# Streaming-window attention and channel mix in one kernel: which units' q and k the crossbar turns, q loaded in 1 KB rows, and new orders

## The chip, the cores and the metric

The kernel runs on one core of one Trainium2 chip. The metric is device time in microseconds (us) of one execution. TensorE (PE) does the matrix products, VectorE (DVE) and ScalarE (ACT) the elementwise work, GpSimd (POOL) small copies and casts. SyncE (SP) issues nearly all DMAs (transfers). PSUM is the memory that PE writes to, in banks; SBUF holds everything else.

## The reference

Two layers, one behind the other. Batch is 4, with 8 heads of width 64 over a sequence of 768, so the model width is 512.

```
scores = q @ k.T / sqrt(64)
keep   = (key < 4) | ((0 <= query - key) & (query - key < 128))
a      = softmax(scores where keep)
x      = a @ v                                   # heads side by side: (4, 768, 512)
x_prev = x shifted by one position, zero at the start
xk     = mu_k * x + (1 - mu_k) * x_prev
xr     = mu_r * x + (1 - mu_r) * x_prev
out    = sigmoid(xr @ w_r) * (relu(xk @ w_k) ** 2 @ w_v)    # w_k: 512 x 1024, w_v: 1024 x 512
```

All inputs and the output are float32; the kernel computes in bf16.

## The kernel before

**Units.** The work is cut into 12 units: unit `u` is batch `u // 3` and 256 positions, T = `u % 3`. For each unit the kernel loads q, k and v, casts them to bf16, turns q and k so that the head width lies on the partitions, makes the scores of two heads at a time (a "chunk"; four chunks), takes the exponential, multiplies by a mask, multiplies by v, divides, mixes with the shifted position, and runs the three products of the channel mix one unit later.

**q and k.** Each is loaded by two DMAs of 256 KB into a float32 buffer (`ks`, `qs`, three of each). There are two ways on from there.

- By PE (the units that are not in `KD` for k, or `QD` for q). The load is in rows of 1 KB: a partition gets four positions that follow one another, as the cut `(w l) (p j) d -> w p l (j d)` with `j=4` says (line 334). After the cast (line 540) PE turns each half of the unit in four 128 x 128 products with an identity (line 573) into a PSUM bank, and ACT or DVE copies the bank to `kt` or `qt` (line 586). That copy reads PSUM with a stride, so that positions come out in order.
- By the crossbar (units in `KD` or `QD`). The load is in rows of 256 bytes, one position per partition (line 314). After the cast (line 533) a transposing DMA for each half, issued by SP, writes `kt` or `qt` (line 559). Nothing is left to PE, ACT or DVE.

If the name stands in `ROWS4`, a unit of the second kind is loaded and cast like one of the first (line 334, 540) and turned by the crossbar; its positions then lie out of order in `qt`, and `block` (line 275) gives the scores a view of it that steps over them: 64 x 4 positions, of which the inner four are 128 elements (256 bytes) apart. Before, `ROWS4` is empty.

**Readers.** `scores` (line 718) uses `kt` as the stationary operand and `qt` as the moving one. The sink scores (line 693) read `qt` too. `sink_keys` (line 667, POOL) copies the first four keys of a batch.

**Other lines.** 498 to 504: casts of the weights; 643: casts of v to `vb`; 772: exponential; 786: mask; 805: values; 819 and 822: division; 846 and 855: turn of x by PE and its copy, units 9 to 11 by transposing DMA (866); 874 and 885: the mix (`td`, `xk`, `xr`); 936: product with w_k; 946, 950: relu; 960, 964: square (`kk`); 976, 982: gate and tanh (`th`); 994, 1003: product with w_v and the output tile `ob`; 906 and 916: the same for the last 128 positions; 1010 and 921: stores. 1014 is a product of a zero tile (`warm`), a "fill": its result is used by nobody.

**What sets the order.** Nothing is scheduled when the kernel is built. Each step is recorded in `P.op` with a number; `ORDER` is a list of these numbers, in which a negative number stands for a fill; `CHOICE` names the engine of every step that can run on more than one; `SLOTS` says which buffer of its pool each tile takes. Each engine runs its instructions strictly in the order in which `ORDER` gives them, POOL and the DMAs in SP's queue too.

Of the kernel before, what the change touches and what calls it, by code (L numbers as in the profile page):

```python
# [18 lines left out]
    90: "ACT", 91: "ACT", 92: "ACT", 93: "ACT", 95: "ACT", 97: "ACT", 99: "ACT", 100: "DVE",  # L19
    103: "DVE", 108: "DVE", 109: "POOL", 111: "DVE", 112: "ACT", 113: "ACT", 139: "DVE", 142:  # L20
    "DVE", 144: "DVE", 145: "DVE", 148: "DVE", 151: "DVE", 154: "DVE", 196: "POOL", 199: "POOL",
    202: "POOL", 206: "DVE", 223: "DVE", 227: "DVE", 228: "ACT", 278: "DVE", 283: "DVE", 284:
    "POOL", 287: "ACT", 288: "DVE", 300: "DVE", 309: "ACT", 313: "ACT", 320: "DVE", 356: "DVE",
    358: "POOL", 363: "POOL", 366: "ACT", 367: "ACT", 369: "DVE", 389: "ACT", 446: "DVE", 447:
    "ACT", 527: "DVE", 548: "ACT", 552: "ACT", 555: "DVE", 560: "ACT", 595: "DVE", 597: "DVE",
    600: "POOL", 602: "DVE", 605: "ACT", 606: "DVE", 628: "ACT", 636: "ACT", 677: "POOL", 681:
    "DVE", 683: "DVE", 684: "DVE", 702: "ACT", 706: "ACT", 710: "ACT", 714: "ACT", 753: "DVE",
    759: "DVE", 761: "ACT", 782: "DVE", 783: "ACT", 787: "ACT", 791: "ACT", 795: "ACT", 832:
    "DVE", 838: "ACT", 839: "ACT", 859: "ACT", 866: "DVE", 867: "ACT", 906: "POOL", 912: "DVE",
    914: "ACT", 915: "DVE", 931: "ACT", 935: "ACT", 939: "ACT", 943: "ACT", 1000: "DVE", 1004:  # L30
    "DVE", 1005: "ACT", 1008: "DVE", 1009: "ACT", 1028: "DVE", 1037: "ACT",
}

KD = range(4, 12)
QD = range(8, 12)
# [13 lines left out]
ROWS4 = ()  # L49
# [134 lines left out]
def kernel(  # L184
# [14 lines left out]
    nc = tc.nc  # L199
# [14 lines left out]
    P = Plan()  # L214
# [164 lines left out]
    warm = tile1([128, 256], BF16, "warm")  # L379
# [689 lines left out]
```

## Time and profile before

| | |
|---|---|
| runs | 167.81, 171.39 and 171.40 us; median 171.39 us |
| profiled execution, first to last instruction (the span) | 167.6 us |
| PE, DVE, ACT, POOL busy | 159.7, 146.2, 133.4, 16.6 us |
| DMA | 34.60 MB in 79042 packets, of which 67112 are under 512 bytes |
| fills (line 1014) | 44 of 512 columns, 13.8 us busy |
| transposing DMAs | 16 of k, 8 of q, 6 of x |

A busy PE is not a PE at its peak: matmuls are pipelined, and the page models their ends. Two things tell more: the pace of a burst of equal matmuls in the chain of waits (the work that ended last, followed back from the end), and the idle time before each group of instructions.

### The profile page before, as it was taken

To read this page: it belongs to the slowest core of one execution; us is meant where nothing else is said; L and a number is where in the kernel's file an instruction comes from. 1 tells how busy PE (TensorE), PEld (TensorE's weight loads), DVE (VectorE), ACT (ScalarE), POOL (GpSimd) and SP (SyncE) were. 2 spreads that over 40 slices of the span, in tenths; PEclk is the share of its full clock that TensorE was granted. 3 is DMA by queue.
4 is the path that set the end of the run, shared out by engine and by line. 5 is a ranking of instruction groups with operands and counts; after the bars stand their busy time and mean duration, and the time that the engine had idled before them with its cause. 6 is when DMAs were issued, how large, how long until landed. Compare 5 with 4: busy or idle time off the path is not lost.

```text
span 167.6 us, 4210 instructions
## 1 busy us (share of the span) xinstructions
PE 159.7 (95%) x1601; PEld 102.4 (61%) x1601; DVE 146.2 (87%) x375; ACT 133.4 (80%) x221; POOL 16.6 (10%) x43
## 2 busy tenths in 40 slices
PE   6999997999999999899999999999999999999991
PEld 1447574755558576676556885665765576764850
DVE  5189999999999999899999999989798799998821
ACT  4269998999999997999879999989799829614340
POOL 6423021005000010022000000010010000000000
PEclk9999999999999999999999999999999999999999
DMA  4999989999899999979999999999997774131303
GB/s 102 300 327 369 346 172 312 372 324 328 189 248 166 204 294 224 253 153 133 218 256 149 214 239 174 233 219 200 211 189 185 194 162 155 63 66 63 125 0 125
DMA packets 79042, 34.60 MB, mean 206 GB/s; under 512 B 67112, under 2 KB 73520, under 8 KB 79024
## 3 DMA queue, kind: packets, MB, share of 16 engines
q1 hardware_dynamic: 79008, 34.35, 92.0%
q8 instruction: 12, 0.20, 0.5%
q14 instruction: 6, 0.05, 0.1%
q10 hardware_dynamic: 16, 0.00, 0.0%
HBM read 24.12 MB, written 6.29 MB: 181 GB/s over the span
## 4 chain that ended last, share of the span: by engine, by line
PE 58%; DVE 11%; DMA 11%; SPq 7%; ACT 7%; issue 3%; ACTq 0%; DVEq 0%
PE bank L936 18%; PE bank L994 18%; PE bank L976 8%; DMA vs<-in_v_dram 6%; SPq L334 5%; PE sc L718 4%; PE bank L805 4%; DMA qs<-in_q_dram 3%; ACT e L772 3%; DMA qt<-qb 2%; DVE ob L1003 2%; DVE e L786 2%; PE bank L846 2%; DVE x L822 2%; PE bank L573 2%
## 5 line engine op out<-in xcount | busy, mean ns | idle before, releaser
L936 PE MATMUL bank<-xk,wk_sb 128*128 128x256 bf16 x384 | 48.1, 273 | 0.1
L994 PE MATMUL bank<-wv_h,kk 128*128 128x512 bf16 x184 | 46.4, 379 | 0.0
L772 ACT ACTIVATE e<-sc 128x1024 bf16<-128x1024 f32 (+1 forms) x48 | 45.4, 974 | 1.2 <-PE sc L718 1.2
L936 PEld LDWEIGHTS <-wk_sb 128*128 128x128 bf16 x384 | 36.2, 98 | 7.6 <-issue 0.7
L786 DVE TENSOR_TENSOR e<-e,mask 128x1024 bf16<-128x1024 bf16 (+1 forms) x48 | 30.7, 655 | 0.7 <-ACT e L772 0.5
L946 ACT ACTIVATE rl<-bank 128x512 bf16<-128x512 f32 x38 | 22.4, 616 | 8.6 <-PE bank L936 8.5
L994 PEld LDWEIGHTS <-kk 128*128 128x128 bf16 x184 | 16.6, 98 | 14.4 <-issue 0.3
L976 PE MATMUL bank<-wr_sb,xr 128*128 128x512 bf16 x96 | 23.8, 379 | 0.0
L885 DVE SCALAR_TENSOR_TENSOR xr<-td,mu_all,xt 128x256 bf16<-128x256 bf16 x48 | 22.5, 482 | 0.0
L885 DVE SCALAR_TENSOR_TENSOR xk<-td,mu_all,xt 128x256 bf16<-128x256 bf16 x48 | 21.3, 477 | 0.1
L964 ACT ACTIVATE kk<-rl 128x512 bf16<-128x512 bf16 x26 | 16.7, 649 | 5.3 <-DVE rl L950 5.3
L822 DVE TENSOR_TENSOR x<-bank,rec 128x256 bf16<-128x256 f32 x48 | 19.2, 416 | 0.3
L1003 DVE SCALAR_TENSOR_TENSOR ob<-th,bank 128x512 f32<-128x512 f32 x23 | 15.7, 681 | 4.2 <-PE bank L994 3.3
L805 PEld LDWEIGHTS <-e 128*128 128x128 bf16 x352 | 14.4, 97 | 5.8 <-DVE e L786 1.0
L805 PE MATMUL bank<-vb,e 128*128 128x65 bf16 x352 | 16.9, 193 | 0.8 <-DVE e L786 0.8
L982 ACT ACTIVATE th<-bank 128x512 f32<-128x512 f32 x24 | 14.3, 616 | 3.6 <-PE bank L976 3.5
L1014 PE MATMUL bank<-warm 128*128 128x512 bf16 x44 | 13.8, 440 | 1.5 <-DVE warm L1032 1.1
L718 PE MATMUL sc<-qt,kt 64*128 64x128 bf16 (+1 forms) x256 | 13.9, 237 | 0.3 <-DMA qt<-qb 0.2
L976 PEld LDWEIGHTS <-xr 128*128 128x128 bf16 x96 | 8.9, 98 | 8.6
L718 PEld LDWEIGHTS <-kt 64*128 64x128 bf16 x256 | 9.3, 94 | 4.5 <-issue 3.0
L874 DVE TENSOR_TENSOR td<-xt 128x512 bf16<-128x512 bf16 x24 | 10.1, 425 | 0.8 <-ACT xt L855 0.8
L855 ACT COPY xt<-bank 128x512 bf16<-128x512 bf16 x15 | 9.1, 608 | 1.8 <-PE bank L846 1.8
(72 smaller groups left out, 157.9 us busy)
## 6 DMA issues: line engine op xcount, KB each, us to landing
vs<-in_v_dram SPq DMA_DIRECT2D x24, 256.0 KB, 5.0
ks<-in_k_dram SPq DMA_DIRECT2D x24, 256.0 KB, 5.6
qs<-in_q_dram SPq DMA_DIRECT2D x24, 256.0 KB, 5.1
out_dram<-ob SPq DMA_DIRECT2D x23, 256.0 KB, 2.9
w<-in_moe_w_k_dram SPq DMA_DIRECT2D x2, 1024.0 KB, 7.3
w<-in_moe_w_v_dram SPq DMA_DIRECT2D x2, 1024.0 KB, 8.6
w<-in_moe_w_r_dram SPq DMA_DIRECT2D x1, 1024.0 KB, 7.1
kt<-kb SPq DMA_TRANSPOSE x16, 4.1
```

The costliest lines, as they stand in the source:

```text
L718: nc.tensor.matmul(out=sc[:, a, o0:o1], lhsT=lhs[rows], rhs=rhs[rows], start=u not in BIAS, stop=True, skip_group_check=u in BIAS)
L772: nc.scalar.activation(out=buf[ek][:, :, lo:], in_=buf[sck][:, :, lo:], func=AF.Exp, scale=scale)
L786: nc.vector.tensor_tensor(out=at, in0=at, in1=m, op=ALU.mult)
L805: nc.tensor.matmul(out=o[:, g, a, :], lhsT=e[:, a, e0:e0 + 128], rhs=rhs, start=(T == 0 and i == 0), stop=(i == len(blocks) - 1), skip_gro ...
L822: P.op("DVE", dve(256), lambda ok=ok, rk=rk, c=c: nc.vector.tensor_tensor(out=buf["x", u][:, :, 128 * c:128 * c + 128].rearrange("p g (a d ...
L885: nc.vector.scalar_tensor_tensor(out=buf[key][:, c, :], in0=buf[tk][:, i, :], scalar=mu[w][:, c:c + 1], in1=xt[:, c, t0 - 1:t0 + 255], op0 ...
L936: nc.tensor.matmul(out=ps[:, i, :], lhsT=wk_sb[:, c, 128 * f:128 * f + 128], rhs=xk[:, c, :], start=(c == 0), stop=(c == NC - 1), skip_gro ...
L946: nc.scalar.activation(out=buf[rk], in_=buf[psk].rearrange("p (i t) -> p i t", i=2), func=AF.Relu)
L964: nc.scalar.activation(out=buf["kk", u][:, 2 * f2:2 * f2 + 2, :], in_=buf[rk], func=AF.Square)
L976: nc.tensor.matmul(out=buf[psk], lhsT=buf["xr", u][:, c, 128 * g:128 * g + 128], rhs=wr_sb[:, c, :], start=(c == 0), stop=(c == NC - 1))
L994: nc.tensor.matmul(out=buf[psk], rhs=wv_h[:, f, :], lhsT=buf["kk", u][:, f, 128 * g:128 * g + 128], start=(f == 0), stop=(f == NF - 1))
L1003: P.op("DVE", dve(512), lambda psk=psk, tk=tk, bk=bk: nc.vector.scalar_tensor_tensor(out=buf[bk], in0=buf[tk], scalar=1.0, in1=buf[psk], o ...
```

## The change

- `KD` goes from units 4 to 11 to units 8 to 11, and `QD` from 8 to 11 to 4 to 11. So k of units 4 to 7 is turned by PE, and q of units 4 to 7 by the crossbar. The numbers of crossbar turns and of PE turns stay the same.
- `ROWS4` goes from empty to `("q",)`: q of units 4 to 11 is loaded in 1 KB rows, turned by the crossbar, and read with the stride by the scores (line 718, 722 in the new file) and the sink scores.
- Fills can now be short: a number from -5 to -8 stands for one of 128 columns. There are 6 of 512 columns and 86 of 128.
- `ORDER`, `SLOTS` and `CHOICE` are new. The first loads now stand in the order k0, q0, v0 (first half), q1, v0 (second half), k1, q2, k2 and v1 by turns, w_k, w_r, k3, q3, v2, w_v. Before, w_k stood ahead of the last load of k2 and of v1.
- By `CHOICE`, POOL casts k 20 times (before 3), q 15 times (7), v 16 times (4), and all of w_k and half of w_r (before none; ACT cast all of w_k). ACT casts k 3 times (15), q 6 (7), v 5 (11), and copies `kt` 12 times (6) and `qt` 5 (14). DVE casts k once (6), q 3 times (10), v 3 times (9), copies `kt` 4 times (2), `qt` 3 (2) and `xt` 5 (3), and does 5 relus (10).

In the new file the lines of the kernel's function stand 4 further down; the fill is at line 1019.

```diff
 CHOICE = {
-    90: "ACT", 91: "ACT", 92: "ACT", 93: "ACT", 95: "ACT", 97: "ACT", 99: "ACT", 100: "DVE",
...
+    90: "POOL", 91: "POOL", 92: "POOL", 93: "POOL", 94: "POOL", 96: "ACT", 97: "ACT", 98: "ACT",
...
-KD = range(4, 12)
-QD = range(8, 12)
+KD = range(8, 12)
+QD = range(4, 12)
...
-ROWS4 = ()
+ROWS4 = ("q",)
...
 ORDER = (
...
 SLOTS = (
...
+        banks = self.pools["bank"]
         for i in ORDER:
             if i < 0:
-                self.fill(self.pools["bank"][-1 - i])
+                self.fill(banks[(-1 - i) % len(banks)], 512 if -i <= len(banks) else 128)
             else:
                 self.ops[i]["emit"]()
...
-    P.fill = lambda bank: nc.tensor.matmul(out=bank, lhsT=warm[:, 0:128], start=True,
-                                           rhs=warm.unsqueeze(1).to_broadcast([128, 2, 256]),
-                                           stop=True)
+    def zeros(bank, n):
+        nc.tensor.matmul(out=bank[:, 0:n], lhsT=warm[:, 0:128], start=True, stop=True,
+                         rhs=warm.unsqueeze(1).to_broadcast([128, 2, 256]) if n == 512 else
+                         warm[:, 0:n])
+
+    P.fill = zeros
```

What the flag `ROWS4` switches on stands in both files:

```
def block(name, u, c, g=None):
    t = buf[name + "t", u]
    if not walked(name, u):
        return t[:, c, :, :] if g is None else t[:, c, g, :]
    t = t.rearrange("p c g t -> p (c g t)").rearrange(
        "p (h j t w) -> p h w t j", h=2, j=4, w=2)[:, c % 2, c // 2]
    return t if g is None else t[:, 32 * g:32 * g + 32]
```

More of the change, by code (lines that the diff above doesn't have):

```diff
@@ L18 @@
 CHOICE = {
-    90: "ACT", 91: "ACT", 92: "ACT", 93: "ACT", 95: "ACT", 97: "ACT", 99: "ACT", 100: "DVE",
[L20 to L30, printed above, removed]
@@ L31 @@
-    "DVE", 1005: "ACT", 1008: "DVE", 1009: "ACT", 1028: "DVE", 1037: "ACT",
-}
-KD = range(4, 12)
-QD = range(8, 12)
+    90: "POOL", 91: "POOL", 92: "POOL", 93: "POOL", 94: "POOL", 96: "ACT", 97: "ACT", 98: "ACT",
+    106: "DVE", 108: "DVE", 109: "DVE", 139: "POOL", 144: "DVE", 145: "POOL", 148: "POOL", 193:
+    "POOL", 196: "POOL", 199: "POOL", 202: "POOL", 205: "DVE", 206: "DVE", 224: "ACT", 228:
+    "ACT", 232: "ACT", 236: "ACT", 275: "POOL", 278: "POOL", 280: "DVE", 281: "POOL", 283:
+    "DVE", 284: "POOL", 286: "DVE", 293: "DVE", 312: "DVE", 317: "ACT", 321: "ACT", 356: "POOL",
@@ new lines @@
+    359: "POOL", 361: "POOL", 364: "POOL", 369: "DVE", 385: "ACT", 389: "ACT", 392: "DVE", 393:
+    "ACT", 436: "POOL", 439: "POOL", 441: "POOL", 443: "DVE", 444: "POOL", 465: "ACT", 473:
+    "ACT", 516: "POOL", 519: "POOL", 526: "ACT", 548: "ACT", 552: "ACT", 556: "ACT", 595:
+    "POOL", 597: "DVE", 598: "POOL", 600: "POOL", 603: "POOL", 605: "ACT", 608: "DVE", 628:
+    "ACT", 632: "ACT", 636: "ACT", 675: "POOL", 677: "DVE", 679: "POOL", 681: "POOL", 683:
+    "ACT", 684: "ACT", 686: "DVE", 710: "ACT", 714: "ACT", 755: "POOL", 757: "POOL", 762: "DVE",
@@ L37 @@
+    774: "DVE", 787: "ACT", 791: "ACT", 830: "POOL", 834: "POOL", 836: "POOL", 839: "ACT", 854:
+    "DVE", 859: "ACT", 866: "DVE", 906: "POOL", 908: "DVE", 910: "POOL", 935: "ACT", 939: "ACT",
+    943: "ACT", 996: "DVE", 1005: "ACT", 1009: "ACT",
+}
+KD = range(8, 12)
+QD = range(4, 12)
 XD = (9,10,11)
```

164 rows, old and new, of tables (ORDER, SLOTS) are left out of this document.

## The prediction

> **What bounds the kernel now.** I read the busy times first, then the stretches of time, then the chain of waits.
>
> ```profile
> span 167.6 us, 4210 instructions
> PE 159.7 (95%) x1601; PEld 102.4 (61%) x1601; DVE 146.2 (87%) x375; ACT 133.4 (80%) x221; POOL 16.6 (10%) x43
> ```
>
> PE looks full, but fills and modelled ends are in that. So I work out what its real work needs, from the pace of bursts in the chain (start, length, what) and the counts of the groups.
>
> ```profile
> L936 PE MATMUL bank<-xk,wk_sb 128*128 128x256 bf16 x384 | 48.1, 273 | 0.1
> L994 PE MATMUL bank<-wv_h,kk 128*128 128x512 bf16 x184 | 46.4, 379 | 0.0
> L976 PE MATMUL bank<-wr_sb,xr 128*128 128x512 bf16 x96 | 23.8, 379 | 0.0
> L805 PE MATMUL bank<-vb,e 128*128 128x65 bf16 x352 | 16.9, 193 | 0.8 <-DVE e L786 0.8
> ```
>
> ```profile
> 12.91 10.07 DMA vs<-in_v_dram
> ...
> 29.64 0.62 PE sc L718 x12
> ...
> 50.64 2.18 PE bank L936 x20
> ...
> 59.51 0.44 PE sc L718 x12
> ...
> 81.59 0.69 DVE ob L1003
> ...
> 97.03 5.09 DMA qs<-in_q_dram
> ...
> 140.01 0.48 PE bank L805 x16
> ...
> 148.68 1.73 PE bank L994 x8
> ...
> 163.89 0.42 DVE ob L916
> ```
>
> One product of 936 takes 2.18 / 20 = 0.109 us, one of 994 or 976 1.73 / 8 = 0.216, one of 805 0.48 / 16 = 0.030, one of 718 0.44 / 12 = 0.037. With the counts: 384 x 0.109 = 41.9, 280 x 0.216 = 60.5, 352 x 0.030 = 10.6, and 256 scores x 0.037 = 9.5. The 168 turns of 128 columns, at the 0.43 ns a column of line 936 (109 ns / 256), make 9.2; for the 116 small products left I put 5. PE needs 137 us of the 167.6. Where are the other 30?
>
> ```profile
> 0.00:12.00 12.00, 10.47 (x53) 4.42 (x54) 5.81 (x22) 4.77 (x8) 5.95 (x24) 1.00 0.84 242
> 12.00:20.00 8.00, 7.92 (x107) 5.27 (x105) 7.65 (x22) 7.89 (x12) 1.57 (x2) 1.00 1.07 362
> 24.00:30.00 6.00, 4.90 (x76) 3.25 (x76) 5.96 (x18) 5.30 (x10) 1.83 (x3) 1.00 0.96 289
> 30.00:60.00 30.00, 30.00 (x317) 19.44 (x312) 29.57 (x75) 29.69 (x52) 2.85 (x5) 1.00 1.13 257
> 80.00:107.00 27.00, 26.79 (x292) 17.59 (x290) 26.30 (x73) 25.12 (x43) 0.00 (x0) 1.00 1.24 211
> 131.00:164.00 33.00, 32.85 (x276) 21.05 (x272) 27.38 (x66) 16.15 (x28) 0.00 (x0) 1.00 0.36 103
> ```
>
> (Columns: stretch, length, busy PE, PE weight load, DVE, ACT, POOL, granted clock, DMA share, GB/s.) And what PE did up to 29.6 us:
>
> ```profile
> L936 PE MATMUL bank<-xk,wk_sb 128*128 128x256 bf16 x32 | 3.8, 272 | 0.0
> L805 PE MATMUL bank<-vb,e 128*128 128x65 bf16 x56 | 2.9, 194 | 0.8 <-DVE e L786 0.8
> L718 PE MATMUL sc<-qt,kt 64*128 64x128 bf16 (+1 forms) x40 | 2.3, 239 | 0.0
> ```
>
> Up to 29.64 that is 32 x 0.109 + 56 x 0.030 + 40 x 0.037 and about 4 of turns: 11 us. **The start** loses 19: v of unit 1, behind w_k in the queue, lands only at 12.91 + 10.07 = 23.0, and then DVE has no idle time (5.96 of 6). **The middle**, 29.64 to 163.9, has 126 us of work in 134.3, so 8 are lost, in a stretch in which DVE (29.57 of 30, 26.30 of 27) and ACT are full as well. **The tail** is 3.7. From 131 on PE alone sets the time.
>
> **The change, part by part.**
>
> *Turns.* PE makes 96 turns of q and k before and after, ACT and DVE copy 24 halves, the crossbar turns 24: no term. Sixteen loads go from 256-byte to 1 KB rows. They are 16 x 0.262 = 4.2 MB; at the 211 GB/s of 80 to 107 that is 19.9 us of the queue, at the 362 of 12 to 20, where long rows prevail, 11.6. Up to 8 us of DMA time go, of which the chain shows 5.1 (q at 97). I count this in the middle, below.
>
> *Fills.* 44 x 0.216 = 9.5 us before, 6 x 0.216 + 86 x 0.055 = 6.0 after, all while PE waits for q, k or DVE: 0. If the shorter ones didn't hold the granted clock (1.00 above), the 11 us of the start would double and reach into the dense part; I allow 3 us for this in the range.
>
> *The start.* v of unit 1 goes from the 17th and 18th place in SP's queue, with two DMAs of 1 MB ahead, to the 14th and 16th with none: 16 x 0.262 = 4.2 MB, which the queue has moved at about 15.6 us (12 us x 242 and 3.6 x 362 GB/s). It waits for nothing then. Late next are the weights and DVE. The second half of w_k ends at 6.3 MB, 21.4 us, and POOL has to cast it. No row shows POOL with 1024 elements; two casts of 512 bound it.
>
> ```profile
> 23.90 0.62 POOL L643 CAST vb<-vs 128x512 bf16<-128x512 f32 x1 [8.07 <-DMA vs<-in_v_dram]
> 25.02 0.81 POOL L643 CAST vb<-vs 128x512 bf16<-128x512 f32 x1
> 25.27 1.09 DVE L786 TENSOR_TENSOR e<-e,mask 128x1024 bf16<-128x1024 bf16 x1
> 39.04 1.70 DVE L786 TENSOR_TENSOR e<-e,mask 128x1024 bf16<-128x1024 bf16 x2
> 39.18 1.02 POOL L540 CAST qb<-qs 128x512 bf16<-128x512 f32 x1 [13.35 <-DMA qs<-in_q_dram]
> ```
>
> So 1.24 to 2.04 us each, the last at 24 to 26, unit 0's product done by about 27. Behind these casts in POOL's queue stand half of w_r and k and q of unit 3, which wait some 6 us; PE has unit 1's product in that time, if DVE has made its `xk`. By the built order DVE has fewer casts and relus ahead of unit 1's last `xk`: adding the durations of their rows, 23.2 us against 27.2. DVE operations overlap by about a tenth, so that is 3.5 less. But POOL now makes 11 short casts and the four long ones up to there, against 6 short; the next part prices these at 0.14 and 0.4, so 2.3 come back. That leaves 1 us, and PE has 0.4 more work done at that point. **-1.4**; from -4 (DVE unhindered) to +1.
>
> *The engines in the middle.* Rows that price the moves:
>
> ```profile
> L643 ACT CAST vb<-vs 128x512 bf16<-128x512 f32 x11 | 7.0, 648 | 1.0 <-DMA vs<-in_v_dram 1.0
> L643 DVE CAST vb<-vs 128x512 bf16<-128x512 f32 x9 | 3.8, 421 | 0.0
> L855 ACT COPY xt<-bank 128x512 bf16<-128x512 bf16 x15 | 9.1, 608 | 1.8 <-PE bank L846 1.8
> L586 ACT COPY qt<-bank 128x512 bf16<-128x512 bf16 x14 | 8.7, 630 | 0.9 <-PE bank L573 0.9
> L855 DVE COPY xt<-bank 128x512 bf16<-128x512 bf16 x3 | 1.2, 415 | 0.0
> L586 DVE COPY qt<-bank 128x512 bf16<-128x512 bf16 x2 | 1.4, 680 | 0.0
> L786 DVE TENSOR_TENSOR e<-e,mask 128x1024 bf16<-128x1024 bf16 (+1 forms) x48 | 30.7, 655 | 0.7 <-ACT e L772 0.5
> ```
>
> DVE loses 18 casts (0.42) and five relus, and gains five copies: 9 us less. ACT loses 19 casts (0.65), four of weights and five copies net, and gains five relus: 16 less. POOL gains 37 casts of 512 and five of 1024. They are not free for DVE: where the cast at 39.18 ran, the pair of masks took 1.70, and the mask at 25.27 took 1.09, against a mean of 0.655; other casts stretched nothing. Over the 13 casts behind the first 10 us I count 1.8 us of stretched DVE operations, 0.14 for each. 42 x 0.14 = 5.9 us come back, so DVE gains about 3 and ACT the full 16. [...] I take **-2.5** of the 8 lost: DVE stays as full, while ACT and DMA waits go. Range 0 to -6.
>
> *The stride.* Units 4 to 11 have six with T > 0 (four chunks x 512 columns, two heads side by side) and two with T = 0 (4 x 384); that they do run side by side shows in the 0.44 us for 2048 columns. With six sink scores of 256 the path holds 16,900 columns read with a step of 256 bytes. No row shows PE with a stride. The nearest are the copies of line 586, which read bf16 from PSUM with a step, against line 855 without: ACT 630 against 608, or 0.04 ns an element; DVE 680 against 415, or 0.52. That is 0.7 us or 8.8 us. [...]
>
> Sum: 167.6 - 1.4 - 2.5 + 0.7 = 164.4 us of span. The runs before lay 0.2 (once) and 3.8 us (twice) above the span, so the same would be 164.6 to 168.2; I put down the middle, 166.4.
>
> **Rivals.**
>
> *The stride costs PE (slower).* PE's moving read behaves as DVE's: 8.8 in place of 0.7, so 164.4 + 8.1 = 172.5 of span, 3% slower. Half of it, 168.1, is within 2%; from about 7.2 on it is slower. [...] Against: the ACT row. Chance 0.28.
>
> *POOL's casts make DVE the bound.* At 0.4 each, 42 casts cost 17 us for the 9 saved: 8 us more DVE. It decides where DVE is full, 30 to 107 us, in which about two thirds of the casts fall: 167.6 + 5.3 - 1.4 + 0.7 = 172.2 at the worst, 169.4 at a cost of 0.3. [...] Against: the mean of 0.14. Chance 0.22.
>
> *The relief is worth more.* The lost 8 us fall to 2 as ACT, DMA and DVE all get room, and the start gains 3: 167.6 - 6 - 3 + 0.7 = 159.3. For it: 5.1 us of DMA and the ACT pieces in the chain between 64 and 107. Against: DVE as full as before. Chance 0.15.
>
> My forecast has 0.35. Some 2% is about what a measurement of this kernel can tell from no change, and 164.2 of span is the line to faster. Faster: half the forecast, the third rival and a little of the others, 0.36. Slower: 0.6 of the first rival, half of the second, and some of a new order gone wrong: 0.32. Within 2%: 0.32. Range: 160 (third rival, runs close to the span) to 174.5 (first rival with 2 us between span and run).
>
> **What would show it.** Bursts of 12 scores of units 4 to 11 at 0.44 to 0.6 us say that the stride is free; near 0.9 that it halves the pace. POOL busy should be about 50 us, the mean mask under 0.75, DVE's total near 145, ACT's near 117. v of unit 1 should land before 18 us, and unit 1's first product of line 940 start before 30. A granted clock under 1.00 before 30 us, DVE over 150 us, or PE idle behind a POOL cast of q or k would make the forecast wrong.

## The result, and the profile after

| | before | after |
|---|---|---|
| median of four runs each | 171.02 us | 194.46 us |
| ratio after / before, 95% interval | | 1.151 [1.139, 1.164] |
| span of the profiled execution | 167.6 us | 194.0 us |
| PE, DVE, ACT, POOL busy | 159.7, 146.2, 133.4, 16.6 us | 182.7, 149.9, 124.2, 47.3 us |
| DMA packets (of these under 512 bytes) | 79042 (67112) | 66756 (50728) |

The change made the kernel 15% slower. The ratio is of runs in the faster of two states alone, and three of the four runs of before lie about 3 us above the fourth, so it is not the quotient of the medians. The prediction said 166.4 us, with a range up to 174.5.

The first page of the profile of after:

```profile
span 194.0 us, 4324 instructions
PE 182.7 (94%) x1649; PEld 109.5 (56%) x1649; DVE 149.9 (77%) x355; ACT 124.2 (64%) x199; POOL 47.3 (24%) x85
```

PE has 23 us more of busy time, while DVE's share fell from 87% to 77% and ACT's from 80% to 64%. So PE itself became slower somewhere. The groups of PE's instructions, each shape apart (shapes and count, then busy us and mean ns of one, then idle time before them), show where. First before:

```profile
L718 PE MATMUL sc<-qt,kt 64*128 64x256 bf16 x96 | 11.6, 272 | 0.3 <-DMA qt<-qb 0.2
L718 PE MATMUL sc<-qt,kt 64*128 64x128 bf16 x160 | 11.1, 216 | 0.0
L693 PE MATMUL bank<-qt,ksink 128*32 128x256 bf16 x32 | 2.3, 282 | 0.6 <-ACT rl L946 0.6
```

The same three groups after:

```profile
L722 PE MATMUL sc<-qt,kt 64*128 64x256 bf16 x96 | 23.5, 500 | 0.3 <-ACT qt L590 0.2
L722 PE MATMUL sc<-qt,kt 64*128 64x128 bf16 x160 | 21.9, 344 | 0.0
L697 PE MATMUL bank<-qt,ksink 128*32 128x256 bf16 x32 | 5.4, 627 | 0.0
```

The counts are the same, the means of the scores are 1.8 and 1.6 times as long, that of the sink scores 2.2 times. These are the products that read q, and they do not wait longer: the idle time before a group is 0.6 us at most before, and 0.3 after. A mean hides that a third of them are of units 0 to 3, read as before. The timeline of PE (start, length, what) shows a burst of the changed units by itself; first one of before, then two of after, with T > 0 (12 products) and with T = 0 (8):

```profile
59.34 0.60 PE L718 MATMUL sc<-qt,kt 64*128 64x256 bf16 x12
```

```profile
62.85 1.92 PE L722 MATMUL sc<-qt,kt 64*128 64x256 bf16 x12
84.29 1.48 PE L722 MATMUL sc<-qt,kt 64*128 64x256 bf16 x8
```

A burst of 12 takes three times as long, although the time of its last product alone, 0.22 and 0.39 us, is in both. Units 4 to 11 have 12 such bursts of 12 and 4 of 8.

The second thing to see is in the start. Stretches of time of after (length, busy PE, PE weight load, DVE, ACT, POOL, granted clock, DMA share, GB/s):

```profile
24.00:30.00 6.00, 3.58 (x60) 2.96 (x58) 5.87 (x10) 2.43 (x5) 4.40 (x6) 1.00 1.14 333
30.00:60.00 30.00, 29.06 (x285) 18.95 (x284) 28.27 (x63) 25.04 (x41) 10.36 (x17) 1.00 0.78 210
60.00:80.00 20.00, 19.63 (x158) 9.99 (x158) 15.46 (x36) 13.48 (x23) 3.35 (x7) 0.91 0.96 220
```

From 24 to 30 us DVE is busy for 5.87 of 6 us, yet it has only 10 instructions there; before it had 18 in 5.96. Its timeline in this stretch, and POOL's beside it:

```profile
23.38 1.56 DVE L790 TENSOR_TENSOR e<-e,mask 128x1024 bf16<-128x1024 bf16 x1
24.86 0.47 DVE L889 SCALAR_TENSOR_TENSOR xk<-td,mu_all,xt 128x256 bf16<-128x256 bf16 x1
25.26 1.25 DVE L889 SCALAR_TENSOR_TENSOR xr<-td,mu_all,xt 128x256 bf16<-128x256 bf16 x1
26.43 1.52 DVE L790 TENSOR_TENSOR e<-e,mask 128x1024 bf16<-128x1024 bf16 x1
```

```profile
22.30 2.09 POOL L508 CAST wk_sb<-w 128x1024 bf16<-128x1024 f32 x2 [2.07 <-DMA w<-in_moe_w_k_dram]
25.03 2.38 POOL L508 CAST wk_sb<-w 128x1024 bf16<-128x1024 f32 x2 [0.63 <-DMA w<-in_moe_w_k_dram]
```

The casts end at 24.39 and 27.41. The masks end at 23.38 + 1.56 = 24.94 and 26.43 + 1.52 = 27.95: both times 0.55 us after the cast. Each of these two masks seems to stand still until the cast is over and then to do its work. Between the two pairs of casts an `xk` takes 0.47, and the `xr` that meets the next cast takes 1.25. The page's group of masks hardly shows this (0.718 us for 0.655 before):

```profile
L790 DVE TENSOR_TENSOR e<-e,mask 128x1024 bf16<-128x1024 bf16 (+1 forms) x48 | 33.3, 718 | 4.7 <-ACT e L776 4.7
```

### The profile page after: what moved, and what is told of

The parts are those of the page before. It is cut to its first block, busy times and chain, and to the rows that moved or that the text cites. A ratio compares the mean times of both kernels' runs of the same rounds, so it can differ in the third digit from the quotient of the medians.

```text
span 194.0 us, 4324 instructions
## 1 busy us (share of the span) xinstructions
PE 182.7 (94%) x1649; PEld 109.5 (56%) x1649; DVE 149.9 (77%) x355; ACT 124.2 (64%) x199; POOL 47.3 (24%) x85
## 2 busy tenths in 40 slices
DMA packets 66756, 34.63 MB, mean 178 GB/s; under 512 B 50728, under 2 KB 61232, under 8 KB 66736
## 4 chain that ended last, share of the span: by engine, by line
PE 73%; DVE 17%; ACT 3%; DMA 3%; issue 2%; SPq 1%; DVEq 0%; ACTq 0%
PE bank L998 19%; PE bank L940 17%; PE sc L722 15%; PE bank L980 9%; PE bank L809 5%; DVE e L790 4%; DVE xk L889 3%; DVE xr L889 3%; DMA qs<-in_q_dram 3%; DVE x L826 2%; PE bank L697 2%; PE bank L1019 1%; DVE td L878 1%; PE bank L850 1%; PE bank L577 1%
## 5 line engine op out<-in xcount | busy, mean ns | idle before, releaser
L950 ACT ACTIVATE rl<-bank 128x512 bf16<-128x512 f32 x43 | 25.0, 600 | 24.8 <-PE bank L940 23.9
L790 DVE TENSOR_TENSOR e<-e,mask 128x1024 bf16<-128x1024 bf16 (+1 forms) x48 | 33.3, 718 | 4.7 <-ACT e L776 4.7
L722 PE MATMUL sc<-qt,kt 64*128 64x128 bf16 (+1 forms) x256 | 33.7, 402 | 0.3 <-ACT qt L590 0.2
L998 PEld LDWEIGHTS <-kk 128*128 128x128 bf16 x184 | 17.3, 99 | 19.6 <-issue 3.4
L889 DVE SCALAR_TENSOR_TENSOR xr<-td,mu_all,xt 128x256 bf16<-128x256 bf16 x48 | 24.4, 536 | 0.0
L889 DVE SCALAR_TENSOR_TENSOR xk<-td,mu_all,xt 128x256 bf16<-128x256 bf16 x48 | 23.2, 512 | 0.5
L722 PEld LDWEIGHTS <-kt 64*128 64x128 bf16 x256 | 11.3, 103 | 19.4 <-issue 14.8
L647 POOL CAST vb<-vs 128x512 bf16<-128x512 f32 x16 | 11.4, 718 | 44.5 <-DMA vs<-in_v_dram 44.0
L823 DVE RECIPROCAL rec<-bank 128x4 f32<-128x4 f32 x48 | 7.9, 174 | 16.3 <-PE bank L809 15.9
L1007 DVE SCALAR_TENSOR_TENSOR ob<-th,bank 128x512 f32<-128x512 f32 x23 | 15.7, 682 | 6.0 <-PE bank L998 2.8
L544 POOL CAST qb<-qs 128x512 bf16<-128x512 f32 x15 | 9.8, 668 | 28.5 <-DMA qs<-in_q_dram 14.2
L809 PEld LDWEIGHTS <-e 128*128 128x128 bf16 x352 | 12.9, 97 | 6.1 <-DVE e L790 2.8
```

The costliest lines, as they stand in the source:

```text
L722: nc.tensor.matmul(out=sc[:, a, o0:o1], lhsT=lhs[rows], rhs=rhs[rows], start=u not in BIAS, stop=True, skip_group_check=u in BIAS)
L790: nc.vector.tensor_tensor(out=at, in0=at, in1=m, op=ALU.mult)
L809: nc.tensor.matmul(out=o[:, g, a, :], lhsT=e[:, a, e0:e0 + 128], rhs=rhs, start=(T == 0 and i == 0), stop=(i == len(blocks) - 1), skip_gro ...
L889: nc.vector.scalar_tensor_tensor(out=buf[key][:, c, :], in0=buf[tk][:, i, :], scalar=mu[w][:, c:c + 1], in1=xt[:, c, t0 - 1:t0 + 255], op0 ...
L950: nc.scalar.activation(out=buf[rk], in_=buf[psk].rearrange("p (i t) -> p i t", i=2), func=AF.Relu)
L998: nc.tensor.matmul(out=buf[psk], rhs=wv_h[:, f, :], lhsT=buf["kk", u][:, f, 128 * g:128 * g + 128], start=(f == 0), stop=(f == NF - 1))
```

## The experiments

Two theories came out of this: the strided read costs PE, and POOL's casts cost DVE. The ratios are against runs of the kernel before on the same chip; their median lay between 168.65 and 169.2 us.

**1. The changed kernel without the stride.** `block` reads 256 neighbouring columns, all else as it was, so the scores are of other rows of q.

```diff
-        "p (h j t w) -> p h w t j", h=2, j=4, w=2)[:, c % 2, c // 2]
-        return t if g is None else t[:, 32 * g:32 * g + 32]
+        "p (h w t) -> p h w t", h=2, w=2)[:, c % 2, c // 2]
+        return t if g is None else t[:, 128 * g:128 * g + 128]
```

> The changed kernel, in which the scores and sink scores of units 4 to 11 read 256 neighbouring columns of qt in place of the strided view (the positions are then out of order, so the output is not the reference's; all instructions, loads, casts, turns and orders stay). Theory 1, the strided read is most of the loss: in the trace of the changed kernel a burst of 12 scores takes 1.52 us with the stride and 0.40 without, one of 8 1.08 against 0.29, and a sink score of 256 columns 0.44 against 0.11; 12 x 1.12 + 4 x 0.79 + 6 x 0.33 = 18.6 us come back, so about 175 us (172 to 177). Theory 2, POOL's casts and the new order hold it back and PE would only wait elsewhere: 185 us or more.

Measured: 174.96 us, ratio 1.039 [1.032, 1.047]. Its bursts:

```profile
66.46 0.61 PE L722 MATMUL sc<-qt,kt 64*128 64x256 bf16 x12
77.53 0.50 PE L722 MATMUL sc<-qt,kt 64*128 64x256 bf16 x8
```

The stride costs 194.46 - 174.96 = 19.5 us. The rows say about the same: 12 x (1.92 - 0.61) + 4 x (1.48 - 0.50) = 19.6 for the scores, and some 3 for the sink scores (5.4 us busy, 2.3 here); PE's busy time fell by 22.3, from 182.7 to 160.4, so about 3 of it cost no time. But 4% stay that the stride does not explain.

**2. The kernel before with the stride in units 8 to 11 alone.**

```diff
-ROWS4 = ()
+ROWS4 = ("q",)
```

> The kernel before with ROWS4 = ("q",) alone: q of units 8 to 11 in 1 KB rows and read with the stride, order, engines and k as before. Six bursts of 12, two of 8 and three sink scores become strided: 6 x 1.12 + 2 x 0.79 + 3 x 0.33 = 9.3 us. Theory 1 (each strided column is paid in full on PE's path): 176 to 181 us. Theory 2 (PE has slack in which half or more of it goes under, and the loss of the change is its order): under 175 us.

Measured: 179.73 us, ratio 1.067 [1.061, 1.072]. Four strided units, with their rows of 1 KB, cost 11.1 us in the order of before, in which POOL casts little. So the new order is not needed for the loss.

**3. Rows of 1 KB alone**: the same, but with the contiguous read of experiment 1, hence other rows of q.

> The kernel before, with q of units 8 to 11 in 1 KB rows as in the third experiment (179.73 us), but the scores read 256 neighbouring columns, so that the result is of permuted rows: the rows alone, in the order of before, without the stride. Theory 1 (the chain's 5.1 us DMA wait for q at 97 us is worth something): 1.5 to 4 us faster than before, ratio 0.975 to 0.99. Theory 2 (the wait is covered by other work that comes later anyway, as the 1.4 us between 1 KB and 256-byte rows in the changed kernel suggests): within 1.4 us of before, ratio 0.99 to 1.008. If it is slower by more than 1%, 1 KB rows cost something themselves.

Measured: 171.45 us, ratio 1.011 [0.999, 1.024]. The gain of 1.5 to 4 us that theory 1 expected isn't there. Whether the rows cost something in that order isn't settled by this interval. The ratio of experiments 2 and 3, 1.067 / 1.011 = 1.055, leaves 9.3 us to the stride of four units, which is the 9.3 worked out ahead of experiment 2.

**4. Eight patterns in one kernel.** In the changed kernel each of units 4 to 11 reads `qt` with another step, so the scores are of other elements of q. It ran once, in 186.0 us; only its bursts are read.

```diff
+        if u in (6, 9):
+            n = {6: 2, 9: 4}[u]
+            t = t.rearrange("p (x w i) -> p w x i", w=2, i=n)[:, w]
...
+        s = {4: 2, 5: 4, 7: 8, 8: 16, 10: 64, 11: 128}[u]
+        t = t.rearrange("p (x s) -> p s x", s=s)[:, s // 2 * w:s // 2 * w + s // 2]
```

> The changed kernel in which each unit from 4 to 11 reads qt with another pattern, 256 columns out of the same 512 (the output is not the reference's): step 4 bytes (unit 4), 8 bytes (5), pairs of neighbours 8 bytes apart (6), 16 bytes (7), 32 bytes (8), runs of four neighbours 16 bytes apart (9), 128 bytes (10), 256 bytes (11). Read from the pace of the bursts, 0.42 ns a column without a stride and 1.73 with 256 bytes. Theory A (a line of 16 bytes needs two hits): steps of 4 and 8 bytes and both runs keep 0.42, steps of 16 and more take 1.73. Theory B (two bf16 come in one word of 4 bytes): every step costs at once, 4 bytes already 0.83 or more, pairs and runs less than steps. Theory C (the cost grows with the step): 16 to 128 bytes lie between.

PE's timeline. The rows are, in this order, units 4, 5, 6, 7, 8, 9 and 10: a step of 4 bytes, of 8 bytes, pairs of neighbours 8 bytes apart (a T = 0 unit, 8 products), steps of 16 and of 32 bytes, runs of four neighbours 16 bytes apart (T = 0), and a step of 128 bytes.

```profile
55.76 0.63 PE L730 MATMUL sc<-qt,kt 64*128 64x256 bf16 x12
...
66.67 1.08 PE L730 MATMUL sc<-qt,kt 64*128 64x256 bf16 x12
...
78.49 0.52 PE L730 MATMUL sc<-qt,kt 64*128 64x256 bf16 x8
...
89.26 1.97 PE L730 MATMUL sc<-qt,kt 64*128 64x256 bf16 x12
...
108.13 2.01 PE L730 MATMUL sc<-qt,kt 64*128 64x256 bf16 x12
...
122.55 0.52 PE L730 MATMUL sc<-qt,kt 64*128 64x256 bf16 x8
...
132.88 1.90 PE L730 MATMUL sc<-qt,kt 64*128 64x256 bf16 x12
```

Beside 0.61 and 0.50 of the contiguous read, three patterns are free, or nearly so: those in which every 16 bytes that are touched hold four used elements, read one after another. Two used elements in 16 bytes cost 0.5 us a burst, one costs 1.3 to 1.4, and a wider step than 16 bytes costs no more. (Unit 11, with four elements 256 bytes apart inside and neighbours outside, took 1.52, for which this gives no reason.) None of the three theories fits whole: two hits in 16 bytes are not enough (A), a step of 4 bytes costs nothing (B), and 32 and 128 bytes cost no more than 16 (C). Unit 11 apart, the price in these bursts goes by how many columns a 16-byte piece yields, up to four; three to a piece was not tried.

**5. The changed kernel mended by that.** The block is read in four runs of 32 with a step of 4 bytes, and the exponential puts the columns back in order, reading PSUM with a step.

```diff
-            "p (h j t w) -> p h w t j", h=2, j=4, w=2)[:, c % 2, c // 2]
-        return t if g is None else t[:, 32 * g:32 * g + 32]
+            "p (h j g t w) -> p h w g j t", h=2, j=4, g=2, w=2)[:, c % 2, c // 2]
+        return t if g is None else t[:, g]
...
+                for a in [slice(0, 2)] if T else [slice(0, 1), slice(1, 2)]:
+                    nc.scalar.activation(
+                        out=buf[ek][:, a, lo:].rearrange("p a (b t j) -> p (a b) t j", t=32, j=4),
+                        in_=buf[sck][:, a, lo:].rearrange("p a (b j t) -> p (a b) t j", t=32, j=4),
+                        func=AF.Exp, scale=scale)
```

> The changed kernel with the same loads and turns, but the block of scores reads its 128 columns as four runs of 32 with a step of 4 bytes inside a run, and the exponential reads PSUM with a step of 32 elements and writes in the true order (two ACT instructions in place of one for the units without T). Theory 1 (PE loses only where fewer than four elements of a 16-byte line are used in a row, as the step pattern of unit 4 showed: 0.415 us for 12 scores): bursts of 12 at 0.40 to 0.45, the time that of the contiguous read plus at most 2 us of ACT, 174 to 178 us. Theory 2 (the step costs PE in the whole kernel even so, or ACT's strided PSUM read becomes the bound): 180 us or more.

Measured: 175.03 us, ratio 1.034 [1.025, 1.042]. The burst:

```profile
66.36 0.63 PE L727 MATMUL sc<-qt,kt 64*128 64x256 bf16 x12
```

The whole loss of the stride is gone with no work left out, and the time shows nothing that ACT would pay for it: an exponential of 1024 columns takes 1.02 us with the step, 1.03 in experiment 1. What is left is the 3 to 4% of the rest. Its runs lay at 175.56 and 174.49 us with a mean granted clock of 1.00, and at 174.49 and 175.79 with 0.98 and 0.97: the clock's falls are not the rest.

**6. POOL writes, but does not read.** Experiment 1 with each of POOL's casts replaced by a copy of its first column and a memset of the whole tile; the casts' values are left out.

```diff
+    def fill_pool(out, in_):
+        one = (slice(None),) + (slice(0, 1),) * (len(out.shape) - 1)
+        nc.gpsimd.tensor_copy(out=out[one], in_=in_[one])
+        nc.gpsimd.memset(out, 0.125)
```

> The changed kernel with the contiguous read of the first experiment (174.96 us there, span 173.3), and each of GpSimd's casts replaced by a copy of its first column and a memset of its whole tile: GpSimd keeps a place in the order and writes the same tiles, but reads almost nothing from SBUF. The casts' values are left out. Theory 1 (what that experiment still loses against before, about 6 us, is DVE's operations stretched beside GpSimd's casts, because both read SBUF): DVE's stretch falls from 12.5 us to 1 to 3, the time falls to 169 to 172. Theory 2 (the casts stretch DVE whatever they read): stretch 8 us or more, time 174 to 176. Theory 3 (the loss is the new order itself, and the granted clock's falls in the start): stretch falls to 1 to 3 us, but the time stays at 173.5 or more.

Measured: 167.88 us, ratio 0.988 [0.983, 0.993]. Busy times of experiment 1, and its mask and `xr` by shape:

```profile
PE 160.4 (93%) x1649; PEld 106.8 (62%) x1649; DVE 151.8 (88%) x355; ACT 122.8 (71%) x199; POOL 52.0 (30%) x85
L889 DVE SCALAR_TENSOR_TENSOR xr<-td,mu_all,xt 128x256 bf16<-128x256 bf16 x48 | 25.1, 550 | 0.0
L790 DVE TENSOR_TENSOR e<-e,mask 128x1024 bf16<-128x1024 bf16 x32 | 24.2, 783 | 0.0
```

The same of this one:

```profile
PE 157.4 (95%) x1649; PEld 106.1 (64%) x1649; DVE 139.8 (84%) x355; ACT 122.3 (73%) x199; POOL 53.9 (32%) x141
L896 DVE SCALAR_TENSOR_TENSOR xr<-td,mu_all,xt 128x256 bf16<-128x256 bf16 x48 | 21.6, 476 | 0.0
L797 DVE TENSOR_TENSOR e<-e,mask 128x1024 bf16<-128x1024 bf16 x32 | 21.0, 683 | 0.0
```

POOL is as busy as in experiment 1, but DVE has 12 us less with the same 355 instructions, and the kernel is 7.1 us faster than experiment 1 (5.2% by the ratios to before, 1.039 / 0.988). Taken operation by operation, against the median of the same shape with no cast beside it, casts stretched DVE by some 12.5 us there, 0.22 for each of POOL's 56, and by nothing here. Theory 1 gave 169 to 172, so even a little more goes than it said. This is also the one kernel of all that stood below before: by 1.2%, too little to count as faster, and with the casts left out.

**7. The same with the stride left in.**

> The changed kernel with its strided read, and GpSimd's casts replaced by a copy of the first column and a memset as in the experiment on writes alone; the casts' values are left out. With the strided read taken away, that replacement was worth 7.1 us (174.96 to 167.88). Theory 1 (the two losses add up: DVE waits for GpSimd whatever PE does): 194.5 - 7.1 = 187.4, so 186 to 189.5. Theory 2 (with the stride PE is the bound nearly everywhere from 40 us on, and only the start pays for the casts): unit 0's product is some 3.5 us earlier, the time 190 to 192. Theory 3 (the stride covers the casts wholly): 193 or more.

Measured: 189.13 us, ratio 1.116 [1.108, 1.124], 5.3 us below the changed kernel. The two losses nearly add up, as theory 1 had it. From 24 to 30 us, changed kernel without POOL's reads:

```profile
24.00:30.00 6.00, 6.00 (x83) 4.93 (x78) 5.88 (x17) 5.15 (x10) 5.08 (x9) 1.00 1.11 323
```

PE has 83 products in place of 60 there. Unit 0's first product with w_k starts at 24.93 us, in the changed kernel at 28.26, after PE has waited 2.32 us for masks: that was the start's loss.

**8. Two attempts to take the casts from POOL** (both with the contiguous read): the five of w_k and w_r to ACT, or all (the second part of the diff).

```diff
-    90: "POOL", 91: "POOL", 92: "POOL", 93: "POOL", 94: "POOL", 96: "ACT", 97: "ACT", 98: "ACT",
+    90: "ACT", 91: "ACT", 92: "ACT", 93: "ACT", 94: "ACT", 96: "ACT", 97: "ACT", 98: "ACT",
...
+        if alts and engine == "POOL":
+            engine = "ACT"
+            cost, emit, port = alts[engine]
```

> The changed kernel with the contiguous read (as e1, not the reference's output), and in it the four casts of w_k and the POOL half of w_r on ACT. In e1 POOL's casts stretched DVE operations by 12.5 us in all, 5.7 of them in the first 36 us, against 1.7 and 0.7 in the kernel before; e1 took 175.0. [...] Theory 2 (w_k lands too late in the new order of loads, whoever casts it): within 1 us of 175.

> As e1, with every cast that POOL made on ACT (56 of them), POOL keeping the masks and the sink keys. ACT was busy 122.8 of 173 us and gets some 37 us more. [...] Theory 2 (the new order and its loads): ACT's casts wait for their loads ahead of exponentials that are ready, 174 us or more.

Measured: 184.13 us, ratio 1.090 [1.082, 1.097], and 237.66 us, ratio 1.40 [1.39, 1.41]. Both are slower than experiment 1. DVE's stretch, counted as in experiment 6, did fall, to some 7 us and to nothing, but in the first run the casts of w_k come late in ACT's queue: PE's weight loads wait for them three times, 7.4 us in all, and the mean granted clock of its runs is 0.94 to 0.96. In the second ACT waits for loads as well (10.7 us for v alone), and the mean clock is 0.88. How the loss divides between these was not tried. Neither run says anything of the stretch's price, only that an order made for one engine doesn't suit another.

**9. Rows of 256 bytes in the changed kernel**, with the crossbar's usual layout (`ROWS4` empty), and with the contiguous read but the load cut as `if by_dma(name, u):`.

> The changed kernel with ROWS4 empty: q of units 4 to 11 loaded in rows of 256 bytes, turned in order and read without a stride, all else as changed. Theory 1 (stride): as the contiguous read, 174 to 178 us, the shorter rows costing 0 to 3 us since the DMA engines have room by then. Theory 2 (the 1 KB rows carry the new order, which needs them in time): 4 us or more above the contiguous read with 1 KB rows.

> As e1, with q of units 4 to 11 loaded in rows of 256 bytes, four heads to a DMA, as the loads of the kernel before did for units 8 to 11 (turns, reads and their order as in e1). The run with ROWS4 empty took 190.5 us, but there the second turn of a unit waited for its scores 5 times, 15.7 us in all. Theory 1 (that wait was its loss): within 2 us of e1's 175. Theory 2 (the long rows are needed in this order): 5 us or more above.

Measured: 190.55 us, ratio 1.133 [1.126, 1.139], and 176.38 us, ratio 1.045 [1.038, 1.051]. The first misses its expectation for a reason of its own, seen in the waits of SP's queue:

```profile
SPq L563 <- PE sc L722: 15.7, 5, 7.4
```

Five times the second turn of a unit's q waits, 15.7 us in all, for the first scores of the same unit. The order was made for the layout of `ROWS4`, in which the first turn brings all that these scores read; here it brings half the positions, and the scores still stand ahead of the second turn, so they read q too early. The second run has no such wait and shows what the rows are worth: 1.4 us, within the intervals.

**10. Fills of 256 columns for 128** (contiguous read).

```diff
-  self.fill(banks[(-1 - i) % len(banks)], 512 if -i <= len(banks) else 128)
+  self.fill(banks[(-1 - i) % len(banks)], 512 if -i <= len(banks) else 256)
```

> As e1, with the 86 short fills at 256 columns in place of 128 (4.7 us more PE work, all before 36 us). In e1 the granted clock fell to a half for 3.4 us twice, at 8.4 and at 28.9, in the kernel before never. Theory 1 (too little PE activity lets the clock fall): no fall, and 1 to 2 us less than 175. Theory 2 (falls don't matter or come from elsewhere): 175 or, as the fills stand ahead of real work, up to 3 more.

Measured: 175.51 us, ratio 1.038 [1.031, 1.045], the same as experiment 1; the one run with a mean clock of 1.00 took 175.45. Neither the short fills nor the clock is a cause of what experiment 1 loses.

**The account.** By ratios: the order and the rows without stride and reads 0.988; POOL's reads 1.039 / 0.988 = 1.052; the stride 1.151 / 1.039 = 1.108. Taken in the other order, the reads cost 1.151 / 1.116 = 1.031 and the stride 1.116 / 0.988 = 1.129. No run that did the whole computation was faster than before.

## Why the prediction was wrong

- **The stride (+0.7 us): this step failed.** It bounded the cost by two copies of line 586 and took ACT's, at 0.04 ns an element. That PE pays for a step as ACT does was the author's estimate, and no run shows it: experiment 1 measured 19.5 us, 19.6 by its bursts. Even the other end, DVE's 8.8 us, was under half. Experiment 4 shows what neither row could tell, as they are of other engines and read PSUM: a burst of 12 takes 0.63 us where 16 bytes of `qt` yield four columns, 1.08 where they yield two, and 1.90 to 2.01 where they yield one, unit 11's 1.52 apart. 0.44 us for 2048 columns of two heads side by side is 0.43 ns a column of each, as for line 936, and the stride takes a whole burst from 0.61 to 1.92.
- **The first rival** had the place and the direction, with under half the price and a chance of 0.28. A step of 4 bytes leaves every second bf16 unread and is free, 0.63 us a burst for 0.61, so leaving elements out does not cost by itself. Nor are two used elements in 16 bytes enough: the step of 8 bytes takes 1.08.
- **POOL's casts (priced at 0.14 each, 5.9 us of DVE).** Without the stride they cost 12.0 us of DVE's busy time, 0.21 each, and 7.1 us of time (experiment 6). In the changed kernel, DVE's busy time is 149.9 us, and 141.3 in experiment 7: 8.6, or 0.15 each, and 5.3 us of time. So the mean was nearly right there; the step that failed was to spread it evenly. About half, 4.6 us by the rows, falls before 36 us, where PE waits for DVE, and a cast of w_k there costs 0.8 to 0.9. The 0.4 of the forecast for such a cast, and of the second rival for all 42, was the author's estimate from the masks at 25.27 and 39.04 (1.09 us, and 1.70 for two, against 0.655 each); no row of before shows a cast of 1024 elements. The mean came from a kernel in which 6 of 13 casts lengthened an operation by over 0.1 us; in the changed kernel 25 of 56 do, in experiment 1 39. Nor was it so that casts "stretched nothing" beside the two pairs shown: of the 1.8 us counted, 0.8 are in those masks, the rest in an `xr`, a square and a `td`. The rival that made DVE the bound allowed 5.3 us. What the runs show of the cause is the two masks that end 0.55 us after a cast, and the memsets of experiment 6, beside which a mask of 1024 columns takes 0.683 us for 0.783.
- **The start (-1.4 us).** DMA did what was forecast: v of unit 1 was cast from 18.13 us on, where before its first cast began at 23.00. But the forecast let POOL's long casts cost DVE 0.4 each, and two of them held masks back by 0.9 and 0.8 (1.56 and 1.52 us, where they take 0.68 in experiment 6). PE had 3.58 us of work from 24 to 30 in place of 4.90, and 6.00 with the reads gone. Unit 1's first product with w_k, expected before 30, starts at 32.90; before it was 30.42, and without the reads 29.73. So 0.7 of the gain was there, and the casts turned it into a loss of 2.5.

```profile
18.13 1.36 POOL L647 CAST vb<-vs 128x512 bf16<-128x512 f32 x2
```

- **The middle (-2.5 us).** DMA was relieved as forecast (12000 packets fewer). ACT's busy time fell by 9 us, to 124.2, where 16 were forecast, for its rows overlap less: their durations add up to 19 us less. Together the relief brought 2.0 us at most, in experiment 6, start included, against 3.9 forecast for both, and there only with DVE freed. Rows alone brought nothing (experiment 3) or 1.4 us (experiment 9).
- **Turns and fills (0).** Experiment 10 agrees for the fills, and the granted clock, for which 3 us of the range were allowed, was 1.00 up to 60 us with the short ones (in experiment 1, with the same fills, 0.86 up to 12 us); the turns weren't tried by themselves.
- **The signs to look for.** Bursts near 0.9 were to speak against the forecast, and they came at 1.92; unit 1's product came too late. Others did not warn: the mean mask of 0.718 stayed under its mark of 0.75, as a mean over 48 hides two of 1.5, and DVE's total of 149.9 lay just at its mark of 150.

## What to carry to other kernels

A product's moving operand in bf16 should yield four elements from every 16 bytes, one after another, as far as these patterns show (0.63 us a burst of 12 for 0.61 contiguous; 1.08 with two, 1.90 to 2.01 with one); a permuted layout is better put right by an engine that reads PSUM anyway, here the exponential, at no cost that showed (175.03 us for 174.96). Work on an idle GpSimd was not free here, where VectorE is dense: its casts took 7.1 us of time without the stride and 5.3 with it. Ask what each cast will hold up, and whether PE waits for that, not how long GpSimd has room. And when no row shows an operation, bounds from rows of other engines and another memory are no bounds; a small change that measures it, or a wider range, is what is left.

## What the runs showed of the hardware that was not expected

- PE read its moving operand at full pace, or nearly so, with a step of 4 bytes (0.63 us a burst of 12 for 0.61), with pairs 8 bytes apart and with runs of four 16 bytes apart (0.52 us a burst of 8 for 0.50). A burst of 12 took 1.08 us with a step of 8 bytes, and 1.97, 2.01, 1.90 and 1.92 with 16, 32, 128 and 256. From its first start to its last that is 0.40 us contiguous and 1.52 with 256 bytes. One pattern of 256 bytes, that of unit 11, lost less (1.52 us a burst), and why is open.
- GpSimd's memsets of the same tiles, with GpSimd as busy as in experiment 1 (53.9 us for 52.0), stretched no DVE operation (a mask of 1024 columns 0.683 us for 0.783, an `xr` 0.476 for 0.550); two masks that ran beside casts took 1.56 and 1.52 us, where they take 0.68, and ended 0.55 us after the cast.
- The granted clock fell in single windows, without the kernel's work changing: in the changed kernel the stretch from 60 to 80 us has a mean of 0.91. Such falls cost nothing that shows in experiment 5, whose runs took 175.56 and 174.49 us at a mean of 1.00, and 174.49 and 175.79 at 0.98 and 0.97.
